# Turning both heads' queries in one group of transposes, with ScalarE writing their high parts twice

## The chip, the cores and the metric

The kernel runs on one core of a Trainium2 chip. The metric is the device time of one execution in microseconds (us); the median of three timed executions is given, and beside it stands one further execution that the hardware profiler recorded. The engines are TensorE (PE in the profile; its weight loads are PEld), VectorE (DVE), ScalarE (ACT), GpSimd (POOL) and SyncE (SP), which issues all DMAs here.

## What is computed

A causal attention with a decay, and then two feed-forward layers, over 4 batches, 8 heads, 576 positions and a head size of 64. All inputs are float32, but the weights of both layers arrive as float64. The reference, cut:

```python
scores = q @ k.T / sqrt(64)
cum    = cumsum(log(clip(f, 1e-4, 1)))
scores = where(causal, -1e9, scores + cum[:, None] - cum[None, :])
attn   = exp(scores - max(scores)); attn = attn / (sum(attn) + 1e-9)
x = (attn @ v)                    # (2304, 512), heads side by side
h = x @ w_in                      # 512 -> 2048
x = (max(h, 0) + alpha * min(h, 0)) @ w_out
h = x @ w2_in
g = where(h >= 1, h, where(h <= -1, 0, (h + 1)**2 / 4))
out = g @ w2_out
```

## The kernel before

**Split numbers.** TensorE multiplies most operands in a 32-bit format of less precision (F32R). The kernel therefore writes a float32 value as a high part (ScalarE casts it) and a low part (VectorE subtracts the high part from the value), and adds up the products of high and low parts in PSUM. For the scores the two parts share one matmul: the 64 features of a head fill only half of the 128 rows, so K lies in SBUF with its high part in one half of the partitions and its low part in the other half, and the queries are laid over both halves. Two matmuls per block of 128 keys (`qk`, L961 to L965) then give the scores: one with the high parts of the queries in both halves, one with their low parts in both halves.

**Stages.** The time of the program falls into three stretches. Up to about 113 us the first batch is treated by a plain routine (`plain_pair`) while the weights of layer 1 are converted from float64. From there to about 542 us batches 1 to 3 are treated as described below, and layer 1 runs on chunks of 256 tokens as soon as the attention has produced them; each of 16 slices of a chunk has a hidden group of 12 matmuls (L1296), two steps on ScalarE and two on VectorE, and an output group of 12 matmuls (L1335). At 542 us the wide slices begin (L1379, L1423), which treat the last 512 tokens of layer 1 together, then layer 2 (L1589, L1574, L1830). The weights of layer 2 are converted on ScalarE and VectorE (L1212 to L1248) once the attention's buffers are free.

**A pair of heads in batches 1 to 3.** Each batch is cut into 256 and 320 queries, and each such unit has 4 pairs of heads, so there are 24 pairs, 12 of each size. For a pair the steps that matter are these.
- SyncE loads K (`load_k`), the queries (`load_q`, L830) and V. The queries land in the single buffer `QR` (L452), a tile of 3 chunks x 2 heads x 2 copies x 64 features, of which the load fills copy 0.
- ScalarE copies copy 0 to copy 1 (`dup_q`, L839), so that a head's 64 features lie twice side by side.
- TensorE transposes K for both heads at once (`ktr`, L863), and ScalarE and VectorE write its high and low halves (`khi` L874, `klo` L877, both 64 partitions high). The transposes of a pair need both buffers of the ring `k`, which are free when the last score matmul of the pair ahead is done.
- For each of the two heads, TensorE transposes the doubled queries, 2 or 3 transposes of 128x128 (`qtr`, L889 to L893), into a PSUM bank of the ring `s`; ScalarE casts all 128 partitions to the high part (`qhi`, L898), and VectorE subtracts for the low part (`qlo`, L901). Head j's two parts take the two slots of the ring `qp`j, so the transposes of head 0 wait for head 0's score matmuls of the pair ahead, and those of head 1 for head 1's.
- The score matmuls, then the bias (L978), mask (L537), maximum (L1023), exponential (L1044), and the product with V (L1078 to L1086).

**What sets the order.** No instruction is reordered on the chip: each engine runs its own queue from front to back. The order of each queue comes from a planner in the kernel (`Order.emit`, L112), which is given tasks with a duration, a due position, the tasks they depend on and the buffers that they take from rings, and which always emits the ready task that can begin first, and among those of one engine the one with the earliest position. Another task or duration anywhere can therefore move instructions on all engines behind it.

## Time and profile before

| | |
|---|---|
| timed executions, us | 1022.03, 1019.96, 1020.40 |
| median, us | 1020.4 |
| profiled execution, us | 1020.85 |
| its span, us | 1018.8 |
| TensorE busy | 999.9 us, 98% |
| VectorE, ScalarE, GpSimd busy | 77%, 63%, 11% |

The span is what lies between the first and the last recorded instruction; 2.05 us of the profiled execution lie around it. Busy shares are averages over the stages, so the profile is to be read by stage: which engine has no gaps there, and what the short gaps of that engine wait for. Matmuls overlap each other in TensorE, so the mean duration of one matmul is longer than the time between the starts of two; where TensorE sets the pace, the chain of waits shows how much time each instruction adds.

### The profile page before, as it was taken

Reading aid. Unit: us, or ns where it says so; the run is one execution under the profiler, and the core shown is the slowest. Engines: PE = TensorE matmul, PEld = TensorE weight load, DVE = VectorE, ACT = ScalarE, POOL = GpSimd, SP = SyncE. Lnnn points to the kernel's source line nnn. Section 1 sums busy time; section 2 is a strip of 40 time slices with the busy share of each in tenths; the row PEclk is TensorE's granted clock in tenths of the full one; section 3 lists DMA queues with packets and bytes.
Section 4 is the critical chain, followed back from the end, with each engine's and each line's share of the span. In section 5 each row is a group of like instructions: output and inputs, shape, how many; then the busy total and the mean of one; then the engine's idle time right before and its main releaser. Section 6 shows DMA issues by size and latency. Waiting matters only on the chain.

```text
span 1018.8 us, 19987 instructions
## 1 busy us (share of the span) xinstructions
PE 999.9 (98%) x6820; PEld 918.1 (90%) x6820; DVE 782.3 (77%) x1898; ACT 646.6 (63%) x1675; POOL 109.4 (11%) x220
## 2 busy tenths in 40 slices
PE   7899999999999999999999999999999999999998
PEld 5788899999999999999998888988889999889886
DVE  8999987887777787787838999987868557565552
ACT  7888788888888888888735655554544235332322
POOL 2000132222322113221100000000000000000000
PEclk9999999999999999999999999999999999999999
DMA  8773223121231212321106667576737544364311
GB/s 267 206 233 106 65 59 77 36 64 37 52 89 37 53 44 46 86 53 38 29 28 198 183 198 230 163 263 239 268 120 255 146 125 122 113 180 124 107 50 62
DMA packets 150452, 123.52 MB, mean 121 GB/s; under 512 B 88096, under 2 KB 120880, under 8 KB 150352
## 3 DMA queue, kind: packets, MB, share of 16 engines
q1 hardware_dynamic: 150352, 122.26, 41.3%
q8 instruction: 54, 0.88, 0.4%
q14 instruction: 46, 0.38, 0.1%
HBM read 93.80 MB, written 28.37 MB: 120 GB/s over the span
## 4 chain that ended last, share of the span: by engine, by line
PE 80%; DVE 7%; ACT 5%; DMA 3%; issue 3%; POOL 1%; SPq 1%; POOLq 0%; ACTq 0%; DVEq 0%
PE ps_z L1574 19%; PE ps_h L1830 12%; PE ps_y L1335 11%; PE ps_h L1296 11%; PE ps_h L1589 7%; PE ps_h L1379 4%; PE ps_y L1423 4%; PE ps_s L964 3%; PE ps_s L642 2%; DVE S L1039 1%; PE ps_o L736 1%; DVE kT L877 1%; PE ps_o L1084 1%; PE pst L713 1%; PE ps_o L1078 1%
## 5 line engine op out<-in xcount | busy, mean ns | idle before, releaser
L1335 PE MATMUL ps_y<-gg,w 128*128 128x256 f32 x1344 | 183.7, 286 | 0.3 <-DVE gg L1318 0.2
L1296 PE MATMUL ps_h<-x,w 128*128 128x256 f32 x1344 | 182.8, 285 | 0.3 <-DVE g L1309 0.3
L1335 PEld LDWEIGHTS ps_y<-gg,w 128*128 128x128 f32 x1344 | 169.1, 190 | 0.9 <-DVE gg L1318 0.7
L1296 PEld LDWEIGHTS ps_h<-x,w 128*128 128x128 f32 x1344 | 168.9, 190 | 0.8 <-DVE g L1309 0.5
L1574 PE MATMUL ps_z<-w,gw 128*128 128x512 f32 x576 | 149.4, 393 | 0.0
L1830 PE MATMUL ps_h<-xc,wc 128*128 128x384 f32 x672 | 136.6, 338 | 0.0
L1830 PEld LDWEIGHTS ps_h<-xc,wc 128*128 128x128 f32 x672 | 121.1, 188 | 10.3
L1574 PEld LDWEIGHTS ps_z<-w,gw 128*128 128x128 f32 x576 | 106.7, 188 | 15.5
L1868 ACT ACTIVATE t<-t,half 128x384 f32<-128x384 f32 x64 | 39.5, 617 | 70.1 <-DVE t L1865 69.7
L1877 ACT CAST gw<-t 128x384 fp32r<-128x384 f32 x64 | 32.7, 512 | 78.9 <-PE ps_z L1574 76.0
L978 ACT ACTIVATE S<-ps_s,nb 128x320 f32<-128x320 f32 (+4 forms) x168 | 75.0, 450 | 9.5 <-PE ps_s L964 8.1
L1309 DVE SCALAR_TENSOR_TENSOR g<-g,calpha,ps_h 128x256 f32<-128x256 f32 x112 | 52.9, 475 | 28.8 <-ACT g L1306 28.2
L964 PE MATMUL ps_s<-q,kT 128*128 128x320 f32 (+4 forms) x336 | 72.1, 298 | 1.1 <-DVE q L901 0.6
L1574 PE MATMUL ps_z<-w,gg 128*128 128x512 f32 x288 | 72.4, 391 | 0.0
L537 POOL TENSOR_SCALAR_AFFINE_SELECT S<-S 128x128 f32<-128x128 f32 (+1 forms) x120 | 41.2, 348 | 250.6 <-ACT S L978 247.0
L1044 ACT ACTIVATE S<-S 128x320 f32<-128x320 f32 (+2 forms) x144 | 60.0, 425 | 12.5 <-DVE S L1039 12.0
L1880 DVE TENSOR_TENSOR gw<-t,gw 128x384 fp32r<-128x384 f32 x64 | 35.5, 555 | 41.0 <-ACT gw L1877 40.7
L1023 POOL PARTITION_ALL_REDUCE pp<-pp x48 | 57.5, 1199 | 56.9 <-ACT pp L1007 24.7
L1318 DVE TENSOR_TENSOR gg<-g,gg 128x256 fp32r<-128x256 f32 x112 | 49.3, 440 | 17.9 <-ACT gg L1315 17.1
L1306 ACT ACTIVATE g<-ps_h 128x256 f32<-128x256 f32 x112 | 42.6, 382 | 30.8 <-PE ps_h L1296 29.1
L1574 PEld LDWEIGHTS ps_z<-w,gg 128*128 128x128 f32 x288 | 53.0, 188 | 9.5
L1039 DVE TENSOR_TENSOR S<-pp,S 128x320 f32<-128x320 f32 (+4 forms) x168 | 57.7, 394 | 3.5 <-POOL pp L1023 2.8
(177 smaller groups left out, 1970.2 us busy)
## 6 DMA issues: line engine op xcount, KB each, us to landing
wc<-wc SPq DMA_DIRECT2D x112, 256.0 KB
raw<-in_moe_w_in_dram SPq DMA_DIRECT2D x32, 512.0 KB
raw<-in_moe_w_out_dram SPq DMA_DIRECT2D x32, 512.0 KB
wc<-sh SPq DMA_DIRECT2D x32, 256.0 KB
wc<-w SPq DMA_DIRECT2D x24, 256.0 KB
out_dram<-osb SPq DMA_DIRECT2D x18, 256.0 KB
qr<-in_q_dram SPq DMA_DIRECT2D x64, 64.0 KB
raw<-in_k_dram SPq DMA_DIRECT2D x32, 128.0 KB
```

The source lines that it names most:

```text
L964: nc.tensor.matmul(out=sb.t[:, :m], lhsT=kt.t[:, kb * P:(kb + 1) * P], rhs=qt[t].t[:, qo:qo + m], start=(t == 0), stop=(t == 1))
L978: nc.scalar.activation(out=Sb.t[:, so:so + m], in_=sb.t[:, :m], func=AF.Identity, bias=bias)
L1023: nc.gpsimd.partition_all_reduce(Mb.t[:, :n], Mx.t[:, :n], P, ReduceOp.max)
L1039: nc.vector.tensor_tensor(out=sl, in0=Mb.t[:, qo:qo + m], in1=sl, op=ALU.subtract)
L1044: nc.scalar.activation(out=Sb.t[:, :gn], in_=Sb.t[:, :gn], func=AF.Exp, scale=-SCALE)
L1296: nc.tensor.matmul(out=hb.t, lhsT=a[:, sl], rhs=b, start=(cc == 0 and t == 0), stop=(cc == NCC - 1 and t == 2))
L1309: nc.vector.scalar_tensor_tensor(out=gb.t, in0=gb.t, scalar=calpha[:, s:s + 1], in1=hb.t, op0=ALU.mult, op1=ALU.add)
L1318: nc.vector.tensor_tensor(out=gg.t[1], in0=gb.t, in1=gg.t[0].bitcast(F32), op=ALU.subtract)
L1335: nc.tensor.matmul(out=Y[c][e // 2][:, e % 2, :], lhsT=a[:, sl], rhs=b, start=(s == 0 and t == 0 and e % 2 == 0), stop=(s == NF - 1 and t ...
L1574: nc.tensor.matmul(out=zb.t, lhsT=a, rhs=b, start=(start and t == 0), stop=(stop and t == 2))
L1589: nc.tensor.matmul(out=hb.t, lhsT=a[:, sl], rhs=b, start=(cc == 0 and t == 0), stop=(cc == NCC - 1 and t == 2))
L1830: nc.tensor.matmul(out=hb.t[:, :m], lhsT=wb.t[:, z, sl], rhs=xb.t[y][:, cc, :], start=(begin and cc == 0 and t == 0), stop=(cc == 1 and t ...
```

## The change

From batch 1 on, `dup_q` is gone, and the query buffer holds each head once. One group of 2 or 3 transposes turns both heads, so that head 0's features come out in PSUM partitions 0 to 63 and head 1's in 64 to 127. For each head ScalarE casts its 64 partitions twice, once to the same half of the query tile (`qhi`) and once to the other half (`qhi2`). VectorE computes the low part for the head's own half only (`qlo`); the other half of the low part is zero, set once by GpSimd when the tile is made (in `second`). So the product of K's low part with the queries' low part is left out of the sum. The rings `qp0` and `qp1` have one slot each, which holds both parts, and the transposes need both rings free, that is, the last score matmul of the pair ahead. The position of these tasks is that of the pair minus one (`QOFF`). The diff, cut to its core:

```diff
+    QOFF = -1
-    R["qp0"], R["qp1"] = Ring(2), Ring(2)
+    R["qp0"], R["qp1"] = Ring(1), Ring(1)
...
-                      ap1.tile([P, 2, NMAX], F32R, tag=f"q{nm}", name=nm))
+                      ap1.tile([P, 2 * NMAX], F32R, tag=f"q{nm}", name=nm))
+            if nm != "m6":
+                z = D - int(nm[1]) * D
+                nc.gpsimd.memset(A1[nm].bitcast(F32)[z:z + D, NMAX:], 0.0)
...
-    QR = [ap1.tile([P, 3, 2, 2, D], F32, name="qr")]
+    QR = [ap1.tile([P, 3, 2, D], F32, name="qr")]
...
-            load_tok(qb_.t[:, :, :, 0, :], q, b, pr, q0, q1)
+            load_tok(qb_.t, q, b, pr, q0, q1)
...
-        def dup_q(qb_=qb_, n=n):
-            t = qb_.t[:, :-(-n // P)]
-            nc.scalar.copy(out=t[:, :, :, 1, :], in_=t[:, :, :, 0, :])
-
-        T["lq"] = add("ACT", act(-(-n // P) * P), dup_q, p0 - 2, [last["lq"]], use=[qb_])
...
+        qx = [Buf(R[f"qp{j}"]) for j in range(2)]
+        def qtr(pb=pb, qb_=qb_, np_=np_, qx=qx):
+            pb.t = ps_a.tile([P, 512], F32, tag=f"s{pb.slot}", name="pst")
+            for j in range(2):
+                qx[j].t = second(f"q{j}")
+            for c in range(np_):
+                nc.tensor.transpose(pb.t[:, c * P:(c + 1) * P], qb_.t[:, c].rearrange("p j d -> p (j d)"), ident)
+
+        pq = p0 + QOFF
+        a = add("PE", 112 * np_, qtr, pq, [last["lq"], last.get("qtr")] + plain_qk[0] + plain_qk[1], new=[pb] + qx, use=[qb_])
         for j in range(2):
-            pb, qb = Buf(R["s"]), [Buf(R[f"qp{j}"]) for _ in range(2)]
...
-                        pb.t[:, c * P:(c + 1) * P], qb_.t[:, c, j].rearrange("p x d -> p (x d)"), ident)
...
-                nc.scalar.copy(out=qb[0].t[:, :n], in_=pb.t[:, :n])
...
-                nc.vector.tensor_tensor(out=qb[1].t[:, :n], in0=pb.t[:, :n], in1=qb[0].t[:, :n].bitcast(F32),
+            def qhi(pb=pb, qb=qx[j], n=n, hr=hr):
+                nc.scalar.copy(out=qb.t[hr, :n], in_=pb.t[hr, :n])
+
+            def qlo(pb=pb, qb=qx[j], n=n, hr=hr):
+                nc.vector.tensor_tensor(out=qb.t[hr, NMAX:NMAX + n], in0=pb.t[hr, :n], in1=qb.t[hr, :n].bitcast(F32),
                                         op=ALU.subtract)
+            def qhi2(pb=pb, qb=qx[j], n=n, hr=hr, lr=slice(D - j * D, 2 * D - j * D)):
+                nc.scalar.copy(out=qb.t[lr, :n], in_=pb.t[hr, :n])
+
+            h = add("ACT", act(n), qhi, pq, [a], use=[pb, qx[j]])
+            h2 = add("ACT", act(n), qhi2, pq, [a, h], use=[pb, qx[j]])
+            qready[j] = [h, h2, add("DVE", dve(n), qlo, pq, [h], use=[pb, qx[j]])]
...
-                                         rhs=qt[t].t[:, qo:qo + m], start=(t == 0), stop=(t == 1))
+                                         rhs=qt.t[:, t * NMAX + qo:t * NMAX + qo + m], start=(t == 0), stop=(t == 1))
```

How the change moves instructions is shown at three places. The line numbers of the changed kernel differ a little from those of the kernel before.

TensorE's queue, before, where the pairs with 256 queries of batch 1 end and those with 320 begin; `ps_s<-q` are score matmuls, `pst<-ident,qr` the transposes of queries, `pst<-ident,raw` those of K, `ps_y` layer 1:

```order
L964 MATMUL ps_s<-q_1876,kT 128x128 x2
L1078 MATMUL ps_o<-S,vF 128x128
L892 MATMUL pst<-ident,qr 128x128 x3
L1335 MATMUL ps_y_2250<-gg,w 128x256 x6
L1335 MATMUL ps_y_2251<-gg,w 128x256 x6
L863 MATMUL pst<-ident,raw_163 128x128 x4
L892 MATMUL pst<-ident,qr 128x128 x3
```

The same place in TensorE's queue, after:

```order
L964 MATMUL ps_s<-q_1773,kT 128x128 x2
L1335 MATMUL ps_y_2308<-gg,w 128x256 x6
L1335 MATMUL ps_y_2309<-gg,w 128x256 x6
L859 MATMUL pst<-ident,raw_164 128x128 x4
L889 MATMUL pst<-ident,qr 128x128 x3
L859 MATMUL pst<-ident,raw_164 128x128
```

One group of query transposes is left of two, and it stands behind the first group of K's.

ScalarE's queue, before, around the copies of queries for the second pair of batch 1; `kT<-pst` are `khi`, `q<-pst` the high parts of queries, `g` and `gg` layer 1, `pp<-S` a copy for the maximum (the copy that doubles these queries, L841, stands further up in the queue):

```order
L1306 ACTIVATE g<-ps_h 128x256
L874 CAST kT<-pst 64x256
L898 CAST q_1808<-pst 128x256
L1007 COPY pp<-S 128x128
L898 CAST q_1876<-pst 128x256
```

The same place in ScalarE's queue, after:

```order
L1306 ACTIVATE g<-ps_h 128x256
L870 CAST kT<-pst 64x256 x2
L898 CAST q_1771<-pst 64x256
L1315 CAST gg<-g 128x256
L905 CAST q_1771<-pst 64x256
L898 CAST q_1773<-pst 64x256
L1007 COPY pp<-S 128x128
L905 CAST q_1773<-pst 64x256
```

Four half-height casts stand where two full-height ones stood, behind both of K's, with other work among them.

VectorE's queue, before, where the attention ends; `x<-pp,x` (L1164) are the last writes of the attention's output, `g<-g,calpha,ps_h` and `gg` are layer 1, once per narrow slice, and behind the last row shown only one copy for layer 2 comes before the last `gg` of the narrow slices:

```order
L1151 TENSOR_TENSOR pp<-pp,m_2326 128x320
L1164 TENSOR_TENSOR x<-pp,x 128x64
L1164 TENSOR_TENSOR x<-pp,x 128x256
L1309 SCALAR_TENSOR_TENSOR g<-g,calpha,ps_h 128x256
L1318 TENSOR_TENSOR gg<-g,gg 128x256
L1309 SCALAR_TENSOR_TENSOR g<-g,calpha,ps_h 128x256
L1318 TENSOR_TENSOR gg<-g,gg 128x256
L1309 SCALAR_TENSOR_TENSOR g<-g,calpha,ps_h 128x256
```

The same place in VectorE's queue, after:

```order
L1151 TENSOR_TENSOR pp<-pp,m_2305 128x320
L1309 SCALAR_TENSOR_TENSOR g<-g,calpha,ps_h 128x256
L1164 TENSOR_TENSOR x<-pp,x 128x64
L1164 TENSOR_TENSOR x<-pp,x 128x256
L1318 TENSOR_TENSOR gg<-g,gg 128x256
L1309 SCALAR_TENSOR_TENSOR g<-g,calpha,ps_h 128x256
L1318 TENSOR_TENSOR gg<-g,gg 128x256
L1309 SCALAR_TENSOR_TENSOR g<-g,calpha,ps_h 128x256
```

The last writes of the attention's output have two narrow slices behind them instead of three.

## Rows read from the trace of the kernel before

**Rows 1.** The page: span, then busy us, share and instructions of the engines.
```profile
span 1018.8 us, 19987 instructions
PE 999.9 (98%) x6820; PEld 918.1 (90%) x6820; DVE 782.3 (77%) x1898; ACT 646.6 (63%) x1675; POOL 109.4 (11%) x220
```

**Rows 2.** Windows by stage, columns in the first row; PEclk is the granted clock's share.
```profile
core 0: us, PE busy (x) PEld busy (x) DVE busy (x) ACT busy (x) POOL busy (x), PEclk, DMA share, GB/s
0.00:113.50 113.50, 103.27 (x1051) 87.58 (x1051) 106.78 (x259) 91.32 (x231) 10.84 (x47) 1.00 0.63 185
113.50:542.00 428.50, 423.61 (x3457) 416.85 (x3452) 327.23 (x888) 344.01 (x1009) 98.60 (x173) 1.00 0.23 56
542.00:1018.80 476.80, 473.04 (x2323) 413.62 (x2321) 348.31 (x753) 211.29 (x440) 0.00 (x0) 1.00 0.54 165
```

**Rows 3.** Windows, sums: around pairs of 256 queries (125-175, 250-300, 400-450), then 320 (175-250, 300-400, 450-500).
```profile
sum 150.00, PE 146.20 PEld 142.47 DVE 116.07 ACT 132.54 POOL 41.91; mean PE 48.73 PEld 47.49 DVE 38.69 ACT 44.18 POOL 13.97
...
sum 225.00, PE 224.04 PEld 221.76 DVE 181.10 ACT 185.76 POOL 53.19; mean PE 74.68 PEld 73.92 DVE 60.37 ACT 61.92 POOL 17.73
```

**Rows 4.** Chain of waits, 478 to 488 us: start, us added, what.
```profile
481.67 1.44 PE ps_h L1296 x12
...
486.88 0.34 PE pst L892 x3
```

**Rows 5.** Groups by shape: query transposes; count | busy us, mean ns | idle before.
```profile
L892 PE MATMUL pst<-ident,qr 128*128 128x128 f32 x120 | 21.1, 274 | 0.2 <-ACT S L978 0.2
```

**Rows 6.** Groups by shape: ScalarE's copies of queries and of K.
```profile
L898 ACT CAST q<-pst 128x320 fp32r<-128x320 f32 x24 | 10.2, 424 | 0.2
...
L874 ACT CAST kT<-pst 64x256 fp32r<-64x256 f32 x24 | 8.7, 364 | 0.8 <-PE pst L863 0.5
L898 ACT CAST q<-pst 128x256 fp32r<-128x256 f32 x24 | 8.7, 371 | 0.3
...
L841 ACT COPY qr<-qr 128x384 f32<-128x384 f32 x12 | 6.2, 513 | 0.0
L841 ACT COPY qr<-qr 128x256 f32<-128x256 f32 x12 | 4.8, 401 | 0.0
```

**Rows 7.** Groups by shape: VectorE's low parts of K and of queries, 256 wide.
```profile
L877 DVE TENSOR_TENSOR kT<-pst,kT 64x256 fp32r<-64x256 f32 x24 | 10.1, 422 | 2.4 <-ACT kT L874 1.8
L901 DVE TENSOR_TENSOR q<-pst,q 128x256 fp32r<-128x256 f32 x24 | 10.0, 421 | 1.7 <-ACT q L898 0.9 <-PE ps_o L1084 0.3
```

**Rows 8.** Groups by shape, then timeline (start, us together): VectorE's subtractions two in a row.
```profile
L1407 DVE TENSOR_TENSOR gL<-g,gH 128x256 fp32r<-128x256 f32 x32 | 12.6, 416 | 0.0
...
L877 DVE TENSOR_TENSOR kT<-pst,kT 64x128 fp32r<-64x128 f32 x24 | 6.9, 288 | 0.5
...
293.73 0.59 DVE L877 TENSOR_TENSOR kT<-pst,kT 64x128 fp32r<-64x128 f32 x2
...
621.07 0.76 DVE L1407 TENSOR_TENSOR gL<-g,gH 128x256 fp32r<-128x256 f32 x2
```

**Rows 9.** GpSimd: groups, the memset of 64x320; timeline, the first mask of batch 1.
```profile
L436 POOL MEMSET qd<- 64x320 f32 x4 | 1.7, 416 | 0.2
...
121.61 0.46 POOL L537 TENSOR_SCALAR_AFFINE_SELECT S<-S 128x128 f32<-128x128 f32 x1 [23.30 <-ACT S L978]
```

**Rows 10.** What TensorE waits for, 113 to 525 us: us in total, times, longest.
```profile
PE ps_o L1084 <- ACT pp L1117: 1.5, 3, 0.7
...
PE ps_s L964 <- DVE q L901: 0.6, 2, 0.3
```

**Rows 11.** Timeline: the attention's last write, and the first wide slice of layer 1.
```profile
535.20 0.73 DVE L1164 TENSOR_TENSOR x<-pp,x 128x64 fp32r<-128x64 f32 x2 [0.31 <-ACT x L1161]
...
542.57 2.91 PE L1379 MATMUL ps_h<-x,w 128*128 128x512 f32 x12
```

**Rows 12.** Timeline: a late weight half of layer 2, and the matmuls that use it.
```profile
659.55 0.68 DVE L1248 TENSOR_TENSOR w<-val,w 128x512 fp32r<-128x512 f32 x1
...
664.43 1.59 PE L1589 MATMUL ps_h<-x,w 128*128 128x256 f32 x12
```

28 lines of the change are left out of this document (8 added, 20 removed).

## The prediction

> **What bounds the kernel now.** I read the page's busy shares first, then a table of windows by stage, then a table that splits the attention stage by how many queries a pair has, then the list of what TensorE waits for, then the costliest groups by shape. TensorE is busy 999.9 of 1018.8 us [rows 1], at the full granted clock (1.00, that is 2.4 GHz) in every stage [rows 2]. The change touches only the stage from 113.5 to 542 us, in which batches 1 to 3 of the attention run between the slices of layer 1; there TensorE is busy 423.61 of 428.50 us, so 4.9 us are idle, while VectorE has 101 us and ScalarE 84 us to spare [rows 2]. After 542 us it is idle 3.8 of 476.8 us [rows 2]. So time taken out of TensorE's stream in the stage should come out of the end, less what becomes idle instead. The idle time is not spread evenly: in three windows around the pairs with 256 queries it is 3.80 of 150 us with ScalarE 88% busy, in the windows around the pairs with 320 queries 0.96 of 225 us with ScalarE 83% busy [rows 3].
>
> **The change, part by part.**
>
> *Transposes.* Each pair now needs 2 (256 queries) or 3 (320) transposes of queries instead of 4 or 6: 12 pairs of each kind, so 60 of 120 go. What one takes out of the stream is its pitch, not its duration: the chain of waits gives three of them 0.34 us before the score matmul behind them goes on [rows 4], 0.113 us each, and 60 x 0.113 = **6.8 us**. The group's busy time, 21.1 us for 120 [rows 5], gives 0.176 us each and 10.5 us; it counts the tails that lie over the next matmul, so it is an upper end. I take 6.8, since the chain is the row in which TensorE itself is the limit. One transpose is shown with 274 ns [rows 5]. [...]
>
> *Score matmuls* keep their number and shapes (the low half is as wide as before, with zeros beside it): nothing.
>
> *ScalarE.* Per pair the copy that doubled the queries and two full-height copies go, and four half-height copies come. Half the partitions cost the same: 364 ns for 64x256 against 371 for 128x256 [rows 6]. With 256 queries: 4 x 364 - (2 x 371 + 401) = 313 ns; with 320, taking 424 for each half copy: 4 x 424 - (2 x 424 + 513) = 335 ns. Over 12 pairs each: 3.8 + 4.0 = **7.8 us more ScalarE work**. A copy that writes into the other half of the partitions is not in the trace for ScalarE; VectorE's is, at no premium (422 ns for such a 64x256 against 421 for the straight 128x256 [rows 7]), so I add none. What of the 7.8 reaches TensorE? At least nothing, since ScalarE has 84 us free; at most all of it. Between the two kinds of window, 5.8 points more of ScalarE go with 2.1 points more of TensorE idle [rows 3], 0.36 per point. The pairs with 256 queries add 3.8 us to 150, 2.5 points, so 2.5 x 0.36% x 150 = **1.4 us**. The other pairs rise from 82.6% to 84.4%, still under the first kind's level, and I count them at nothing; by the same slope they would be another 1.5 us, kept for the range.
>
> *VectorE.* The two low parts go from full to half height at the same price (421 against 422 ns [rows 7]). They no longer overlap their neighbours: two half-height subtractions of 288 ns take 0.59 us, two full ones of 416 ns 0.76 us [rows 8], so the second pair overlaps by 0.07 us and the first does not. The Trainium skill (VectorE: DVE Perf Modes, § Two Vector instructions with no wait between them) says an instruction is held until all earlier ones finish when its inputs or output start in another 32-partition quadrant than the last ones; head 1's low part now starts at partition 64, so it and its successor would be held, a rule against this change. By the rows that is 2 x 24 x 0.07 = 3.4 us of VectorE, hidden in its 101 us of spare time [rows 2]; without that cover it would stand on the same path as ScalarE's share.
>
> *GpSimd.* Two memsets of 64x320, once: such a memset is 416 ns, and GpSimd stood idle 23.3 us in front of the first mask of batch 1 [rows 9]. Nothing; without that gap 0.8 us. *DMA:* the same transfers; the one query buffer is free after one group of transposes, and the doubling copy no longer stands between load and transpose. The list of what TensorE waits for in the stage names no query load [rows 10], so no gain is counted.
>
> *The new wait.* The joint transposes need both heads' buffers, so they stand behind the previous pair's last score matmul; before, head 0's stood ahead of it in 14 of 23 pair boundaries. Behind the waiting transposes TensorE's queue holds layer-1 matmuls, in groups of 12, and who waits for them is the pair's first scores. But K's transposes always stood behind that same score, in both orders, and K's copies are longer. Between the last score of a pair and the first of the next the orders have 84 layer-1 groups before and 86 after, over 23 boundaries, never fewer than 2, and a group is 1.44 us [rows 4]. All waiting on a query's low part is 0.6 us today [rows 10]. Counted at nothing; K hides it.
>
> *What is late next.* The last attention matmul now stands one hidden-layer group nearer to the wide slices that end layer 1 (six left instead of seven), and on VectorE the last write of the attention's output has two narrow slices behind it instead of three. Its slack today is from 535.93 to 542.57, 6.6 us [rows 11]; one slice, two groups of 1.44 us, comes off, and 3.7 us stay. The layer-2 weights start to be converted behind that write, so they shift by the same 2.9 us against TensorE. There VectorE is full: the last weight half that layer 2 needs early starts at 659.55, takes 0.68 and is used at 664.43 [rows 12], 4.2 us of slack, 1.3 left. Nothing, with 1.5 us for the range.
>
> **Sum.** -6.8 + 1.4 = -5.4 us. The profiled execution took 1020.85 us, a span of 1018.8 and 2.05 around it, and lies 0.45 above the median of the three timed runs; carried over to that median: 1020.4 - 5.4 = **1015.0 us**.
>
> **Rivals.**
> - *The 256-query pairs lose all their cover:* ScalarE's 3.8 us there become TensorE idle, 1020.4 - 6.8 + 3.8 = 1017.4. For it: nearly all idle time lies there. Against: even there ScalarE is free for 17 of 150 us [rows 3].
> - *The converted weights come late:* the 1.3 us of slack go, and 2 to 3 us of the gain are waited out in layer 2's first chunk: about 1017.5.
> - *ScalarE is the true bound:* all 7.8 us arrive, 1020.4 - 6.8 + 7.8 = 1021.4, no change. Against: its 84 idle us.
> - *Slower: the boundary is exposed.* Place: the first score matmul after each pair boundary. The two further copies per pair stand ahead of it in ScalarE's queue: 12 x 2 x 0.364 + 12 x 2 x 0.424 = 18.9 us if all show, 1032.5; it turns slower once more than some 9 us show, that is, once the query copies end later than K's and the two to six groups between don't cover them. For it: in ScalarE's new order the query copies come after K's and other work stands among them. Against: 0.6 us of such waits now.
> - *Each transpose frees its whole 274 ns:* 60 x 0.274 = 16.4, so 1020.4 - 16.4 + 1.4 = 1005.4. Against: the chain's 0.34 us for three.
>
> **How the numbers follow.** Forecast 0.62, first rival 0.16, weights 0.04, ScalarE 0.08, boundary 0.08, whole transposes 0.02. A measurement of this kernel can tell about 0.2%, 2.0 us, from no change, so faster means under 1018.4: 0.62 + 0.16 + 0.04 + 0.02 = 0.84; the same 0.08; slower 0.08. The range reaches up to 1018.4, which takes in the first two rivals and the slope's second share, and down to 1012.0, which is the forecast with no idle added (1013.6) and the 1.6 us of today's idle gone that stand behind query and output copies in the list of waits (two of its rows, 0.6 and 1.5, less a part that will stay).
>
> **What would show it.** Right: 60 query transposes instead of 120 at about 0.113 us in the chain; ScalarE about 7 to 8 us busier in the stage, the cross-half copies at 364 to 424 ns; the stage's TensorE busy time 6 to 8 us less, and its idle time 5 to 7 us; the stretch from the first wide slice to the end as long as before (476 us). Wrong: cross-half copies well over 0.42 us; waits of the first scores on the query copies by more than 3 us in all; TensorE waiting around layer 2's first chunk; idle time over 9 us in the stage, above all around the 256-query pairs.

## The result, and the profile after

The changed kernel takes 1028.84 us (median of six runs, 1027.66 to 1031.71) against 1020.18 us before: ratio 1.0082, 95% interval 1.0066 to 1.0098. By the ratio that is 8.4 us slower, where the forecast was 5.4 us faster and its range ended at 1018.4. The profiled execution took 1031.24 us, a span of 1029.5. Of the runs below one execution of `two_banks` and one of `casts_kept` took more than 5500 us, and the figures given for these two leave it out.

The page's span and engine shares of the kernel after, which answer to [rows 1]:

```profile
span 1029.5 us, 19904 instructions
PE 1002.4 (97%) x6760; PEld 916.4 (89%) x6760; DVE 787.6 (77%) x1898; ACT 660.6 (64%) x1699; POOL 110.9 (11%) x222
```

TensorE issues 60 matmuls fewer, and is not less busy for it. ScalarE's own busy time is up by 13.9 us, VectorE's by 5.3 us. The same three stages as in [rows 2], cut at the first transposes of K in batch 1 and at the first wide slice:

```profile
core 0: us, PE busy (x) PEld busy (x) DVE busy (x) ACT busy (x) POOL busy (x), PEclk, DMA share, GB/s
0.00:115.40 115.40, 107.14 (x1051) 90.75 (x1051) 107.05 (x259) 91.61 (x230) 11.87 (x52) 1.00 0.61 182
115.40:552.30 436.90, 422.44 (x3397) 412.78 (x3394) 333.45 (x890) 358.54 (x1035) 99.05 (x170) 1.00 0.23 55
552.30:1029.50 477.20, 472.81 (x2318) 412.87 (x2316) 347.05 (x752) 210.42 (x438) 0.00 (x0) 1.00 0.54 165
```

The stage in the middle of the kernel before, cut at the same two places:

```profile
113.60:542.60 429.00, 424.11 (x3458) 417.39 (x3455) 327.73 (x890) 344.51 (x1009) 98.60 (x173) 1.00 0.23 56
```

The last stage is 1.0 us longer. The first one is 1.8 us longer, but its length wanders between 112.0 and 115.9 us over all the kernels below, those in the arrangement of before among them, so nothing is built on that. The stage in the middle is where the change acts: 429.0 us became 436.9, and TensorE's idle time in it 4.9 became 14.5. TensorE's busy time in it fell by 1.7 us, where 6 to 8 were forecast.

What TensorE waits for in that stage, beside [rows 10] (us in total, times, longest):

```profile
PE ps_s L964 <- DVE q L901: 6.4, 12, 1.7
PE ps_s L964 <- ACT q L905: 2.2, 4, 1.0
...
PE ps_o L1084 <- ACT pp L1117: 1.0, 2, 0.7
```

L964 is the score matmul, L901 the queries' low part, L905 ScalarE's second, cross-half cast. The page's rows of all score matmuls, before and after (count | busy us, mean ns | idle time ahead, and what ended most of it):

```profile
L964 PE MATMUL ps_s<-q,kT 128*128 128x320 f32 (+4 forms) x336 | 72.1, 298 | 1.1 <-DVE q L901 0.6
...
L964 PE MATMUL ps_s<-q,kT 128*128 128x320 f32 (+4 forms) x336 | 73.0, 300 | 10.0 <-DVE q L901 6.4
```

The wait that the forecast counted at nothing is there. One such place in the timeline, at the start of a 320-query pair (start, us together, what; in brackets the idle time ahead and what ended it):

```profile
209.38 0.50 PE L889 MATMUL pst<-ident,qr 128*128 128x128 f32 x3
...
213.18 1.40 DVE L873 TENSOR_TENSOR kT<-pst,kT 64x128 fp32r<-64x128 f32 x3
...
214.28 0.85 ACT L898 CAST q<-pst 64x320 fp32r<-64x320 f32 x2
215.14 0.87 ACT L905 CAST q<-pst 64x320 fp32r<-64x320 f32 x2
...
215.61 0.42 PE L964 MATMUL ps_s<-q,kT 128*128 128x320 f32 x1 [0.98 <-ACT q L905]
216.04 0.48 DVE L901 TENSOR_TENSOR q<-pst,q 64x320 fp32r<-64x320 f32 x1 [1.46 <-PE ps_s L964]
216.57 0.71 PE L964 MATMUL ps_s<-q,kT 128*128 128x320 f32 x3 [0.55 <-DVE q L901]
```

Both heads' queries lie in one PSUM bank, and head 0's low part starts here only when all four casts that read this bank are over: VectorE stands still for 1.46 us in front of it, and TensorE twice. The transposes were done at 209.88 us, but ScalarE, busy with other work, came to the first cast 4.4 us later, and three layer-1 groups had gone by before the score. K's last low part ended at 214.58, head 0's low part of the queries 1.94 us after it. In 18 of 24 pairs head 0's low part began after the fourth cast, in 10 of them within 0.06 us of its end; in the kernel before it began before the other head's cast had ended in 21 of 24. From there a natural story is: TensorE's idle time before score matmuls rose from 1.1 to 10.0 us, and that is the loss. The runs below contradict it.

### The profile page after: what moved, and what is told of

Its sections match the earlier page's. It is cut to its first block, busy times and chain, and to the rows that moved or that the text cites. A ratio compares the mean times of both kernels' runs of the same rounds, so it can differ in the third digit from the quotient of the medians.

```text
span 1029.5 us, 19904 instructions
## 1 busy us (share of the span) xinstructions
PE 1002.4 (97%) x6760; PEld 916.4 (89%) x6760; DVE 787.6 (77%) x1898; ACT 660.6 (64%) x1699; POOL 110.9 (11%) x222
## 4 chain that ended last, share of the span: by engine, by line
PE 76%; DVE 13%; ACT 6%; issue 3%; DMA 1%; POOL 0%; SPq 0%; POOLq 0%; DVEq 0%; ACTq 0%
PE ps_z L1574 19%; PE ps_h L1830 12%; PE ps_y L1335 11%; PE ps_h L1296 10%; PE ps_h L1589 6%; PE ps_h L1379 4%; PE ps_y L1423 4%; PE ps_s L964 3%; DVE raw L1229 2%; DVE w L1248 1%; DVE raw L1234 1%; PE ps_o L1078 1%; PE ps_o L1084 1%; DVE st L660 1%; DVE kT L873 1%
## 5 line engine op out<-in xcount | busy, mean ns | idle before, releaser
L964 PE MATMUL ps_s<-q,kT 128*128 128x320 f32 (+4 forms) x336 | 73.0, 300 | 10.0 <-DVE q L901 6.4
L964 PEld LDWEIGHTS ps_s<-q,kT 128*128 128x128 f32 x336 | 53.8, 191 | 14.9 <-DVE q L901 7.3
```

What stands on the lines that cost most here:

```text
L964: nc.tensor.matmul(out=sb.t[:, :m], lhsT=kt.t[:, kb * P:(kb + 1) * P], rhs=qt.t[:, t * NMAX + qo:t * NMAX + qo + m], start=(t == 0), stop= ...
```

## The experiments

Times are medians beside the kernel before, run in turn on the same chip (1019.8 to 1021.5 us each time). Where terms are added up, each is a ratio times 1020.2 us.

### First round: four edits that the planner answered with another order

Four theories of the loss are tried. Theory A: the shared bank, in which the first low part waits for all four casts. Theory B: the joint transposes stand behind head 1's last score, so the first scores of the next pair come too soon after them. Theory C: ScalarE's added work. Theory D: the order of work alone.

`two_banks`, a bank for each head, at one time:

```diff
-        pb = Buf(R["s"])
+        pbs = [Buf(R["s"]) for _ in range(2)]
...
-            for c in range(np_):
-                nc.tensor.transpose(pb.t[:, c * P:(c + 1) * P], ...
+            for j in range(2):
+                for c in range(np_):
+                    nc.tensor.transpose(pbs[j].t[:, c * P:(c + 1) * P], ...
```

> The changed kernel, but each head's transposes go into a PSUM bank of their own again (120 transposes instead of 60, about 6.8 us of TensorE time back by the prediction's own price), still all at one time behind both heads' last scores, and still with ScalarE's four casts. Theory A (one bank: head 0's low part stands behind all four casts because they read one bank): the low part now waits for two casts; the 10.0 us that TensorE idled before score matmuls fall to about 5, and the time is 1028.8 + 6.8 - 5 = about 1030 to 1031. Theory B (joint time: the transposes stand behind head 1's last score, and whatever comes behind them is uncovered): the idle stays at 10, 1028.8 + 6.8 = 1035.6. Theory C (ScalarE's added work alone): also 1035.6. Theory D (no cause in the pairs, only another order of work): anything within some 3 us of 1035.6 with idle before scores not related to the casts.

`before_joint`, the kernel before with both groups of transposes in one task:

```diff
-            a = add("PE", 112 * np_, qtr, pos_of(2 * pr + j) - 1, [T["lq"], last.get("qtr")] + plain_qk[j], new=[pb] + qb,
+        a = add("PE", 112 * np_ * 2, qtr, p0 - 1, [T["lq"], last.get("qtr")] + plain_qk[0] + plain_qk[1],
+                new=pbs + qx[0] + qx[1], use=[qb_])
```

> The kernel before, with one edit: both heads' transposes (still 120, still two banks, still the duplication on ScalarE and one cast and one low part for each head) stand together, behind both heads' last scores and both heads' buffers, as the changed kernel's do. Theory A (one bank): the low part still waits for its own cast only; idle before score matmuls stays near the 1.1 us of before, up to 3; 1020 to 1022. Theory B (joint time): the idle goes to 8 to 10 us and the time to 1028 to 1030. Theory C (ScalarE's added work): nothing is added, 1020.2. Theory D (order): 1020.2 give or take 3.

`from_sbuf`, the second cast from SBUF, and the planner told so:

```diff
-                nc.scalar.copy(out=qb.t[lr, :n], in_=pb.t[hr, :n])
+                nc.scalar.copy(out=qb.t[lr, :n], in_=qb.t[hr, :n].bitcast(F32))
...
-            h2 = add("ACT", act(n), qhi2, pq, [a, h], use=[pb, qx[j]])
+            h2 = add("ACT", act(n), qhi2, pq, [a, h], use=[qx[j]])
```

> The changed kernel with ScalarE's second cast of each head reading the first cast's result in SBUF instead of the PSUM bank: the same number of ScalarE instructions, but the low parts need not stand behind the second casts. Theory A (one bank): head 0's low part is ready two casts (0.84 us) sooner in about half of the pairs; idle before scores falls from 10 to 4 to 6 us and the time to 1022 to 1025. Theory B (joint time): the first score is still behind the transposes and the chain, idle 8 to 10, 1027 to 1029. Theory C (ScalarE's work): same work, 1028.8. Theory D (order): 1028.8 give or take 3.

`margin1000`, queries counted as ready 1000 ns later in the plan:

```diff
+        qready = [x + [add(f"X{j}", 1000, lambda: None, pq, x)] for j, x in enumerate(qready)]
```

> The changed kernel with the planner alone told otherwise: it counts a head's queries as ready 1000 ns later than the end of their last cast and low part, so it puts other TensorE work ahead of the first scores; no instruction is added or removed, and every other rule of the plan is unchanged. Theories A and B (the first scores wait for the queries): idle before scores falls from 10 to under 3 us, the time to 1019 to 1022, which is 6 to 9 under the changed kernel. Theory C (ScalarE's work delays other readers): the waits on ScalarE stay, 1027 to 1029. Theory D (order): 1028.8 give or take 3, with no relation to the idle before scores.

Measured: 1050.31 (ratio 1.0309), 1035.47 (1.0150), 1034.22 (1.0142) and 1048.49 us (1.0277). All four are beyond every number that was named. In `margin1000` the idle time before scores did fall from 10.0 to 2.5 us, as A and B asked, and the kernel became 20 us slower. What TensorE waits for after 400 us in `two_banks` shows one part of why:

```profile
PE ps_h L1380 <- ACT x L1162: 6.2, 1, 6.2
```

L1380 is the first wide slice of layer 1, and it waits for the attention's last output. The planner, told of longer waits, had placed its other TensorE work earlier; the attention's last score ended at 546.5 us instead of 511.9, with too little left to cover its tail. The same wait is 6.2 us in `before_joint` and 5.6 in `margin1000`, and none in the kernels before and after. The granted clock is another part; the middle stage of `two_banks`, then of `margin1000`:

```profile
112.70:563.50 450.80, 434.85 (x3470) 426.23 (x3467) 336.00 (x885) 360.10 (x1030) 96.16 (x173) 0.98 0.21 48
...
115.60:563.90 448.30, 429.90 (x3410) 420.43 (x3407) 332.17 (x885) 360.90 (x1030) 99.21 (x170) 0.97 0.21 48
```

At 0.98 and 0.97 that is some 9 and 13 us by estimate (0.02 of 450.8 and 0.03 of 448.3). These runs tell that an order planned anew costs more than what was to be measured. They don't tell A from B. All further runs but the last two keep every instruction that they share with their parent in its order on every engine: only what an instruction reads, whether it is there, or (once) on which engine it runs is changed.

### Is it the scores' wait? Take it away

`after_free` and `before_free`: the scores take keys instead of queries.

```diff
-                                         rhs=qt.t[:, t * NMAX + qo:t * NMAX + qo + m], start=(t == 0), stop=(t == 1))
+                                         rhs=kt.t[:, qo:qo + m], start=(t == 0), stop=(t == 1))
```

> The changed kernel, every instruction in the same order on every engine, but the score matmuls of the batches from the second on take keys in the place of queries as their moving operand (same size, same type; so the scores are not the reference's). Transposes, casts and low parts of the queries still run; nothing waits for them. Theory A/B (the first scores of a pair wait for that pair's queries): the 10.0 us of idle before score matmuls go, and with them what the clock lost: 1015 to 1019. Theory C (ScalarE's added work): the casts still run, 1026 to 1029. Theory D (the order that the planner writes for the changed tasks is a longer one, waits or not): 1024 to 1029.

> The kernel before with the same edit, in its own order: score matmuls take keys in the place of queries. The trace of before showed 1.07 us of idle before score matmuls: all theories give 1018.5 to 1020.2. The difference to the changed kernel under the same edit is then what 60 transposes less and the other order are worth without the query wait: theory A/B say 4 to 6.8 us in favour of the changed kernel, theory D 4 to 9 us against it.

Measured: 1029.41 (1.0083, 1.0061 to 1.0104) and 1020.16 us (1.0002, 0.9991 to 1.0012). Nothing came back. The groups of the score matmul and of one that follows, in `after_free` (count | busy us, mean ns | idle ahead, and what ended it):

```profile
L964 PE MATMUL ps_s<-kT 128*128 128x320 f32 (+4 forms) x336 | 69.5, 294 | 7.0 <-DVE q L901 4.6 <-ACT g L1306 0.8 <-ACT q L905 0.7
L1084 PE MATMUL ps_o<-PH,vH 128*128 128x320 f32 (+1 forms) x96 | 30.7, 320 | 3.7 <-ACT PH L1054 2.1 <-ACT pp L1117 1.3
```

A score no longer reads queries, yet 4.6 us of its idle time still end with a query's low part: scores and transposed queries take turns in a ring of three banks, and the low part is the last reader of the bank that the score is to write. Another part moved on to the value matmuls, behind ScalarE. So this run took the direct wait away and not the bank's; it did show that idle time before one kind of matmul is no price. It moves.

`sbuf_kept`: the same line as in `from_sbuf`, the planner not told, so that the order stays.

> The changed kernel, every instruction in the same order on every engine; only ScalarE's second casts read the first cast's result in SBUF instead of the PSUM bank, so that head 0's low part need not stand behind them. Theory A (one bank): idle before scores falls from 10.0 to 5 to 8 us and the time to 1023 to 1027. Theory B (joint time) and C (ScalarE's work): 1028.8. Theory D (order): the order is the same, so 1028.8.

Measured: 1029.13 us (1.0074, 1.0050 to 1.0098), as the changed kernel. The row of its score matmuls:

```profile
L964 PE MATMUL ps_s<-q,kT 128*128 128x320 f32 (+4 forms) x336 | 71.9, 299 | 7.7 <-DVE q L901 4.7
```

The idle time before scores fell from 10.0 to 7.7 us, so the low parts did come sooner; the time did not fall. Theory A, in the form that the four casts in one bank are the price, is not borne out; a part of up to some 3 us is not excluded by the intervals.

`hold_free`: casts and low parts read the untransposed queries in SBUF, so that the bank is free at once.

```diff
-                nc.scalar.copy(out=qb.t[hr, :n], in_=pb.t[hr, :n])
+                nc.scalar.copy(out=qb.t[hr, :n], in_=flat(qb_)[hr, :n])
```

> The changed kernel, every instruction in its order; the queries' casts and low parts read the untransposed tile in SBUF in the place of the PSUM bank (same shapes, same count; the values are not the queries' transposes), and the scores wait for them as before. The bank is free as soon as the transposes are done and the casts need not wait for the transposes. Theory A: idle before scores falls from 10.0 to under 4 us, 1016 to 1021. Theory C (ScalarE's and VectorE's work is the same): 1027 to 1030. Theory D: 1027 to 1030.

Measured: 1081.93 us. It tells nothing on the bank: there is one tile of untransposed queries, the casts now hold it longer, and the next pair's load waits. What ScalarE waits for:

```profile
ACT q L901 <- DMA qr<-in_q_dram: 23.8, 14, 2.7
```

### Is it the order, or the casts? Leave the casts out

`after_none` and `before_none`: as the two above, and no casts and no low parts of queries.

```diff
             def qhi(pb=pb, qb=qx[j], n=n, hr=hr):
-                nc.scalar.copy(out=qb.t[hr, :n], in_=pb.t[hr, :n])
+                pass
```

> The changed kernel with every remaining instruction in its order, but without the queries' casts and low parts of the batches from the second on (96 half casts, 37.3 us of ScalarE, and 48 low parts, 21.5 us of VectorE, are left out; the score matmuls take keys as their moving operand). The joint transposes stay; their bank is free as soon as they are done. Theory A (the queries' one bank is held by casts and low parts, and scores wait for it or for them) and theory C (ScalarE's added work): 1010 to 1016, idle of TensorE between 113 and 555 us down from 14 to under 6 us. Theory D (the order written for the changed tasks is itself the longer one): 1024 to 1029, the idle stays above 10 us.

> The kernel before with the same left out (48 full casts, 16.6 us of ScalarE, and 48 low parts, 19.9 us of VectorE; the 24 duplications and 120 transposes stay; score matmuls take keys). All theories: 1016 to 1020, since TensorE idled only 4.9 us in that stage. What tells is the changed kernel under the same edit minus this one: theories A and C say -4 to -7 us (60 transposes), theory D +4 to +10 us.

Measured: 1009.27 (0.9896, 0.9873 to 0.9919) and 1017.25 us (0.9963, 0.9948 to 0.9979): by the ratios, the changed kernel is 6.8 us under the kernel before when both lack the queries' casts. So its transposes and its order together are worth what was forecast, or nearly (within some 3 us), and theory D, that the new order is longer by itself, falls. The middle stage of `after_none`, then of `before_none`:

```profile
112.10:530.20 418.10, 414.81 (x3396) 410.21 (x3395) 311.56 (x842) 323.38 (x938) 98.83 (x170) 1.00 0.23 57
```

```profile
115.50:539.30 423.80, 421.66 (x3455) 416.92 (x3454) 310.83 (x842) 331.64 (x961) 99.58 (x173) 1.00 0.24 57
```

TensorE idles 3.3 and 2.1 us. With the casts and low parts put back, the kernel before grows by 3.8 us and the changed one by 19.0. That is where the gain went, and more.

### Which part of the casts?

Theory C again, ScalarE's amount of work, against a theory E: the length of the chain of casts and low parts from the transposes to the first score.

`casts_kept`: the kernel before, in its order and with its own banks and times, but ScalarE casts each head twice, the second time across the halves; no duplication.

```diff
-                nc.scalar.copy(out=qb[0].t[:, :n], in_=pb.t[:, :n])
+                for r in (j, 1 - j):
+                    nc.scalar.copy(out=qb[0].t[r * D:(r + 1) * D, :n], in_=pb.t[j * D:(j + 1) * D, :n])
...
-            nc.scalar.copy(out=t[:, :, :, 1, :], in_=t[:, :, :, 0, :])
+            pass
```

> The kernel before in its own order, with ScalarE's new work alone: no duplication; each head's transposes (still 120, still at each head's own time and in its own bank) turn both heads' queries, ScalarE casts the head's half twice, the second time across the halves, and VectorE takes the low part of that half beside zeros. ScalarE gains 48 half casts of 0.39 to 0.42 us and loses 24 duplications, some 10 us of work, and each low part stands behind two casts instead of one. Theory C (ScalarE's work): 1026 to 1029, with idle of TensorE behind ScalarE. Theories A, B and D: 1020 to 1023, since the bank is not shared, the time is not joint, and the order is that of before.

`casts_sbuf`: the same, the second cast from the first one's result.

> The kernel before in its own order with the two half casts, the second one from the first one's result in SBUF: the low part waits for one cast again and runs beside the second one; only the score waits for both. Theory E: the chain is cast, then the longer of cast and low part, which is that of before; 1019 to 1023. Theory C (the work is the same as with both casts from the bank): 1027 to 1030.

`load_only`: the kernel before, its full casts and low parts, no duplication, and a half copy behind each cast into a tile that nothing reads.

```diff
                 nc.scalar.copy(out=qb[0].t[:, :n], in_=pb.t[:, :n])
+                nc.scalar.copy(out=spare[(1 - j) * D:(2 - j) * D, :n], in_=qb[0].t[j * D:(j + 1) * D, :n].bitcast(F32))
```

> The kernel before in its own order, with ScalarE's added work and without its place in the chain: no duplication (each head's transposes turn both heads' queries, so the scores are not the reference's), the full cast and the full low part as before, and behind each full cast a half cast of 64x320 or 64x256 from SBUF into a spare tile that nothing reads. ScalarE's work is then 18.7 us more and 8.5 us less, 10 us more, as in the kernel before with the two half casts (1029.6), but no low part and no score waits for it. Theory C (amount of ScalarE's work): 1027 to 1030. Theory E (chain from transposes to first score): 1018 to 1022.

Measured: 1029.07 (1.0086, 1.0062 to 1.0110), 1029.32 (1.0077, 1.0059 to 1.0095) and 1029.82 us (1.0076, 1.0055 to 1.0097). All three are the same: whether the low part waits for the second cast, only the score does, or nobody does, makes no difference that was measured. ScalarE's work alone, in the order of before, costs 7.8 us (5.6 to 10 by the interval). The middle stage of `load_only`, beside [rows 2]:

```profile
112.30:548.40 436.10, 427.09 (x3457) 418.10 (x3454) 328.95 (x890) 359.05 (x1034) 98.92 (x173) 1.00 0.23 55
```

ScalarE is busy 359.05 of 436.10 us, which is 82%, up from 80%, and still 77 us free by the sum. Its busy time rose by 14.5 us (344.5 in the stage cut the same way), the stage by 7.1. The chain of work that ended last changed too. The page's shares of it by engine, first before, then `load_only`, then `after_none`:

```profile
PE 80%; DVE 7%; ACT 5%; DMA 3%; issue 3%; POOL 1%; SPq 1%; POOLq 0%; ACTq 0%; DVEq 0%
```

```profile
PE 69%; DVE 13%; ACT 9%; DMA 4%; issue 3%; SPq 1%; POOL 0%; ACTq 0%; DVEq 0%; POOLq 0%
```

```profile
PE 92%; ACT 3%; DVE 2%; DMA 2%; issue 1%; SPq 0%; POOL 0%; POOLq 0%; ACTq 0%; DVEq 0%
```

These shares are of the whole span, and they mislead. The fall from 80% to 69% lies in the first stage and the last one, which hold none of the added copies: TensorE's part of the chain is 79.2 and 469.7 us there before, 19.3 and 410.6 in `load_only`. The pieces of the chain that lie in the middle stage, added up by engine (us):

| Kernel | stage | TensorE | ScalarE | VectorE |
|---|---|---|---|---|
| `before_none` | 423.8 | 389.5 | 15.0 | 5.1 |
| `after_none` | 418.1 | 373.7 | 19.6 | 16.3 |
| before | 429.0 | 269.3 | 47.4 | 62.5 |
| `load_only` | 436.1 | 279.7 | 85.3 | 36.9 |
| after | 436.9 | 301.2 | 53.3 | 51.0 |

Without the queries' casts and low parts the chain of this stage is some 90% TensorE. In the kernel before it is 63%, so more than a third of it ran through other engines already, which the 4.9 us of idle time don't tell. The added copies leave TensorE's part about as it was and raise ScalarE's from 47.4 to 85.3 us. Where several waits end at nearly the same time the chain shows one of them only, so it tells the way of the loss and not its size.

`no_second_kept`: the changed kernel without the second casts. `no_low_kept`: without the low parts. In each the line of the instruction is `pass`.

> The changed kernel, order kept, without the second casts (the other half of each high tile stays zero, so the product of the keys' low parts with the queries is left out): two casts and two low parts on the bank, 18.7 us less on ScalarE, and nothing in their place. Theory C: under the kernel before, 1012 to 1018. Theory E: the head's low part still stands behind two casts and starts only behind the joint transposes; 1022 to 1028. The kernel with GpSimd's second copy was 1028.0; what this one is under that is the price of GpSimd's copy as a link.

> The changed kernel, order kept, without the queries' low parts (left zero, so that product is left out): four casts on the bank, VectorE has 21.5 us less. Theory E with the low part as the last link (the waits named VectorE's low part in 12 of 16 cases): 1013 to 1018. Theory C: 1025 to 1030.

`pool2_kept`: the second casts on GpSimd.

```diff
-                nc.scalar.copy(out=qb.t[lr, :n], in_=pb.t[hr, :n])
+                nc.gpsimd.tensor_copy(out=qb.t[lr, :n], in_=qb.t[hr, :n].bitcast(F32))
```

> The changed kernel, order kept; the second, cross-half copy of each head is made by GpSimd from the first cast's result in SBUF, so ScalarE loses 48 half casts (18.7 us) and the bank has two casts and two low parts to wait for. Theory C: ScalarE then has less to do than in the kernel before; 1015 to 1020. Theory A: the bank is held for some 0.8 us less, but the first score now waits for GpSimd's copy (not seen in a trace; half to twice a ScalarE copy of the same shape, 0.2 to 0.8 us): 1021 to 1027. Theory D: 1027 to 1030.

Measured: 1021.68 (1.0014, 0.9998 to 1.0029), 1023.00 (1.0008, 0.9994 to 1.0023) and 1028.00 us (1.0077, 1.0050 to 1.0103). Taking out the second casts gives 6.9 us back, the low parts 7.5. Neither brings the kernel below the kernel before. The middle stage of `no_second_kept`:

```profile
112.80:544.50 431.70, 421.24 (x3397) 412.43 (x3394) 333.43 (x890) 341.57 (x986) 99.17 (x170) 1.00 0.23 55
```

ScalarE has 3 us less to do there than in the kernel before, TensorE 60 transposes fewer, and the stage is still 2.7 us longer. So ScalarE's amount of work is not all of it: one cast and one low part for each head cost the kernel before 3.8 us, and in the joint arrangement 12.0. They are not the same amount of busy time: in the stage ScalarE's rose by 12.9 us in the one and by 18.2 in the other, VectorE's by 16.9 and 21.9. At `load_only`'s 7.1 us of stage for 14.5 of ScalarE, the 5.3 us more would be 2.6 of the 8.2, by estimate.

`pool2_kept` has the same relief on ScalarE and none of the gain. GpSimd's copies take 481 ns each, and wait in front of its masks and reductions:

```profile
POOL q L905 <- ACT q L898: 49.9, 19, 6.6
```

A queue that was idle for long stretches in sum had its work behind that wait. Whether that, or the first scores' wait for the copy, makes the 6.4 us was not separated.

### Does the place behind the last score cost it?

Theory F says so: standing behind head 1's last score, the queries' chain is left uncovered.

`no_low_double` and `double_full`: two buffers for a pair's queries, so that the transposes can stand ahead of the previous pair's last scores.

```diff
-    R["qp0"], R["qp1"] = Ring(1), Ring(1)
+    R["qp0"], R["qp1"] = Ring(2), Ring(2)
...
-                qx[j].t = second(f"q{j}")
+                qx[j].t = second(f"q{j}")[:, qx[j].slot * NMAX:(qx[j].slot + 1) * NMAX]
```

and in `double_full` besides (with one slot instead of two in the ring of row sums, to make room)

```diff
+                    nc.tensor.matmul(out=sb.t[:, :m], lhsT=kt.t[rows, kb * P:(kb + 1) * P],
+                                     rhs=ql.t[rows, qo:qo + m], start=False, stop=True)
```

> The changed kernel without the queries' low parts (the second score matmul takes the high part again, same size), as the run before it, but the two heads' high parts have two buffers each, in the memory of the low parts. The order is planned anew: in all 23 later pairs the joint transposes stand 8 to 48 rows of TensorE's order ahead of the previous pair's last score, where they stood 2 to 10 rows behind it. Theory F (the place behind the last score leaves the queries' chain uncovered): 6 us or more under the 1023.0 of the kernel without low parts, 1010 to 1017, idle before scores under 2 us. Theory C (only ScalarE's amount of work counts; it is the same): 1020 to 1025.

> The changed kernel with nothing left out and two buffers for a pair's queries: high parts of both heads two slots each, and the low parts of both heads in one tile of two slots (head 0 in the lower, head 1 in the upper partitions), which the second score matmul takes with 64 rows in the place of 128 rows half of which were zero; so that it fits, the ring of row sums has one slot instead of two. Order planned anew. Theory F: the chain is covered again, what remains is ScalarE's added work and 60 transposes less; 1014 to 1021, which may be under the kernel before. Theory C: the work is the same, 1026 to 1031. If 64-row matmuls or the one slot cost something of their own, above either.

Measured: 1025.79 (1.0037, 1.0021 to 1.0052) and 1138.00 us (1.1134). In `no_low_double` the transposes stand 8 to 48 rows ahead, and idle time before scores fell from 4.0 to 1.9 us; the idle time of the stage stayed (9.3 and 9.5), and the time did not come down from 1023.0. Theory F is not borne out. As the order was planned anew it is not refuted either: the first round shows what that alone can do.

`double_full` has a loss of its own. Its second score matmul, over 64 rows (L965), and its first (L963), then two stretches of 100 us with the granted clock:

```profile
L963 PE MATMUL ps_s<-q,kT 128*128 128x320 f32 x72 | 28.3, 393 | 2.8 <-DVE kT L871 2.8
...
L965 PE MATMUL ps_s<-ql,kT 64*128 64x320 f32 x72 | 32.8, 456 | 0.0
```

```profile
300.00:400.00 100.00, 93.05 (x589) 82.92 (x589) 54.18 (x146) 61.59 (x173) 14.88 (x27) 0.85 0.18 40
400.00:500.00 100.00, 90.77 (x545) 77.96 (x543) 60.46 (x160) 70.55 (x199) 19.37 (x36) 0.86 0.17 39
```

Over its middle stage of 538.0 us the granted clock was 0.92, which by estimate is some 43 of the 116 us. Whether the 64-row matmuls, the one slot of row sums or the new order brought the loss was not separated.

None of the changed versions that compute the scores in full is under the kernel before.

## Why the prediction was wrong, step by step

The loss can be put together from runs that keep their order, each a difference of two ratios times 1020.2 us:

| Term | from | us |
|---|---|---|
| 60 transposes and 24 duplications fewer, the new order | `after_none` less `before_none` | -6.8 |
| one cast and one low part per head, in the joint arrangement | `no_second_kept` less `after_none` | +12.0 |
| the same in the arrangement of before | before less `before_none` | -3.8 |
| the second casts | after less `no_second_kept` | +6.9 |
| sum, before rounding | | +8.4 |

That the sum comes out at the measured +8.4 is no test, since every other kernel stands in it once with each sign; the table shows where the loss lies. Each term has an uncertainty of some 2 to 3 us, from the intervals. The lengths of the middle stage give -5.7, +13.6, -5.2 and +5.2, together +7.9.

- **Transposes: right, as far as measured.** Sixty fewer, and -6.8 us where nothing else hides it. The 24 duplications that went too and the new order are in that figure; no run shows the transposes apart. The group has half the count and half the busy time:

```profile
L889 PE MATMUL pst<-ident,qr 128*128 128x128 f32 x60 | 10.6, 274 | 0.0
```

  The Trainium skill (TensorE: Matmul & The Clock Gate, § Part 4: PE-mode transpose) gives about 275 ns for a transpose; the trace agrees with 274 ns as the duration. A forecast that frees that much for each was a rival, and the measured 6.8 us, with its 3 us of uncertainty, leave out its 16.4 us.

- **ScalarE: the step that failed.** Its prices were right: the copies of [rows 6] have these successors, and the cross-half cast (L905) has no premium.

```profile
L898 ACT CAST q<-pst 64x320 fp32r<-64x320 f32 x24 | 10.1, 421 | 0.4
L905 ACT CAST q<-pst 64x320 fp32r<-64x320 f32 x24 | 10.1, 420 | 1.6 <-DVE q L901 1.2
L898 ACT CAST q<-pst 64x256 fp32r<-64x256 f32 x24 | 8.8, 367 | 0.4
L905 ACT CAST q<-pst 64x256 fp32r<-64x256 f32 x24 | 8.8, 367 | 1.1 <-DVE q L901 0.7
```

  In the groups' busy times that is 37.8 us instead of 29.9, as forecast (+7.9 beside +7.8). But durations of neighbours overlap, and ScalarE's own busy time rose by 13.9 us: the size was off by nearly a factor of two. And what of it reaches the end was forecast as 1.4 of 7.8, 18%; `load_only` measured 7.8 us for 13.5 us more of ScalarE's busy time over the span, 58%. The slope it was taken from compared two kinds of stretch at one load of ScalarE each; it doesn't tell what more load does. Nor does taking work away: `before_none` leaves out 12.9 us of ScalarE's busy time and 16.9 of VectorE's in the stage and gained 3.8 us. "84 us free" is a sum over the stage; in the chain of that stage ScalarE and VectorE have 5 to 9% without the queries' casts and low parts, 26% before and 28% in `load_only`, so their work takes turns with TensorE's.

- **The new wait: "counted at nothing; K hides it" failed too.** The first scores did wait: the idle time before score matmuls is 10.0 us instead of 1.1, and 8.6 of it ends with a query's low part or second cast, where more than 3 was named as a sign of being wrong. The layer-1 groups between were counted rightly, but only against the copies' own durations: in the place at 214 us ScalarE came to the casts 4.4 us after the transposes, behind other work, and the queries were ready 1.94 us after K. The price is another matter: a shorter chain on the bank (`sbuf_kept`) and scores that need no queries (`after_free`) brought nothing back that was measured. What the joint arrangement costs with single casts is measured, 12.0 - 3.8 = 8.2 us. Which of its links it is (the transposes' place, the casts and low parts behind other work, the greater busy time, the bank in the ring of three) stays open.

- **VectorE:** the low parts kept their prices, 421 and 489 ns beside 421 and 486, and VectorE's busy time rose by 5.3 us where 3.4 were forecast. The Trainium skill (VectorE: DVE Perf Modes, § Two Vector instructions with no wait between them) has an instruction held when its partitions begin in another quadrant than those of the one ahead; that speaks for a rise, and no run here shows it apart. "Hidden in its 101 us of spare time" is the same mistake as with ScalarE: without the low parts VectorE is busy 20.6 us less, and the time is 7.5 us shorter (`no_low_kept`).

- **GpSimd and DMA: right; the tail: more slack than computed.** Nothing of GpSimd or the DMAs shows in the kernel after. The attention's last write and the first wide slice of layer 1 in the kernel after:

```profile
546.15 0.56 DVE L1164 TENSOR_TENSOR x<-pp,x 128x64 fp32r<-128x64 f32 x2
...
552.34 2.91 PE L1379 MATMUL ps_h<-x,w 128*128 128x512 f32 x12
```

  The write ends at 546.71 us, so 5.6 us of slack are left, where 3.7 were computed. In three kernels of the first round, whose attention ends later, the wide slices wait 5.6 to 6.2 us.

- **Rivals.** "ScalarE is the true bound" (1021.4) had the mechanism and too small a size. "The boundary is exposed" named the side and the place; its wait is in the trace, but that the wait is itself the price is not borne out. The idle time was looked for around the 256-query pairs. It came around the others: in the windows of [rows 3] 4.3 of 150 us beside 9.6 of 225. ScalarE's work alone, in `load_only`, does add it around the 256-query pairs, 6.3 of 150 beside 2.2 of 225; so most of the idle time around the others comes only with the joint arrangement. The kernel after, then `load_only`:

```profile
sum 150.00, PE 145.74 PEld 142.78 DVE 115.79 ACT 131.74 POOL 43.62; mean PE 48.58 PEld 47.59 DVE 38.60 ACT 43.91 POOL 14.54
...
sum 225.00, PE 215.37 PEld 209.60 DVE 180.81 ACT 192.43 POOL 50.29; mean PE 71.79 PEld 69.87 DVE 60.27 ACT 64.14 POOL 16.76
...
sum 150.00, PE 143.71 PEld 138.44 DVE 114.67 ACT 134.53 POOL 40.12; mean PE 47.90 PEld 46.15 DVE 38.22 ACT 44.84 POOL 13.37
...
sum 225.00, PE 222.76 PEld 219.66 DVE 178.90 ACT 190.63 POOL 53.01; mean PE 74.25 PEld 73.22 DVE 59.63 ACT 63.54 POOL 17.67
```

## What to carry to other kernels

Here an engine at 80% beside one at 99% was not free, since the two hand work to each other in turns. Before adding work to such an engine, add as much work that nothing waits for, with the order kept, and see what the time does. Leaving work out is no substitute: the casts and low parts were worth 3.8 us when they were left out of the kernel before, and added copies cost 7.8. Idle time in front of one instruction is not its price; take the wait away and see whether the idle time moves elsewhere. Where a planner writes the order, an experiment has to keep that order, or it measures the planner.

## What the hardware showed that was not expected

After the stall at 214 us the granted clock fell. The windows of the kernel after, 2 us each:

```profile
214.00:216.00 2.00, 1.02 (x6) 0.56 (x4) 0.54 (x2) 1.93 (x6) 0.00 (x0) 1.00 0.45 107
216.00:218.00 2.00, 1.45 (x9) 1.19 (x8) 1.90 (x5) 1.54 (x6) 0.00 (x0) 1.00 0.15 46
218.00:220.00 2.00, 2.00 (x11) 1.99 (x11) 1.92 (x5) 1.90 (x5) 0.02 (x1) 0.55 0.01 4
220.00:222.00 2.00, 2.00 (x12) 2.00 (x11) 0.80 (x3) 0.48 (x2) 0.27 (x1) 0.59 0.00 0
222.00:224.00 2.00, 2.00 (x19) 2.00 (x18) 1.08 (x4) 1.95 (x6) 0.76 (x3) 1.00 0.00 0
```

TensorE was busy 2.47 of 4 us, and the next 4 us were granted 0.55 and 0.59 of 2.4 GHz, near the lower of its two levels, 1.2 GHz, while it was fully busy; by estimate 1.7 us more were lost that way (4 x 0.43). The clock is not the cause of the loss: in the middle stage of `load_only` it was 1.00, and the time was as long.

In `double_full` a matmul over 64 rows was not cheaper than one over 128 but dearer (456 against 393 ns at 320 columns), and in two stretches that held them the granted clock was 0.85 and 0.86 with TensorE 91 to 93% busy; whether the rows or the idle time brought the clock down was not separated.
